# A fused attention and gated-MLP kernel on one NeuronCore: gated tiles' differences shared by two engines and stored a period later, weight sums made early, seven products in another order

## The chip, the cores and the metric

One NeuronCore of a Trainium2 chip runs the whole kernel in one launch. The metric is the device time of one execution in microseconds, lower is better. The engines have in-order queues of their own: TensorE (PE in the profile; PEld is its weight load), VectorE (DVE), ScalarE (ACT), GpSimd (POOL) and SyncE (SP), which issues nearly all DMAs.

## The reference

The output mixes an attention branch and a gated MLP of the same input `x` (2048 tokens, 512 features; 32 heads of 16; hidden width F = 1792), weighted by a gate per token:

```python
def _A_ref(x, wqkv, wo):
    ...
    scores = jnp.einsum("bhqd,bhkd->bhqk", q, k) * scale
    p = _softmax(scores, axis=-1)
    o = jnp.einsum("bhqk,bhkd->bhqd", p, v)
    return (lambda x, *d: x.transpose(*d))(o, 0, 2, 1, 3).reshape(B, S, D) @ wo

def _B_ref(x, w_gate, w_up, w_down):
    g = jnp.einsum("bsd,df->bsf", x, w_gate)
    u = jnp.einsum("bsd,df->bsf", x, w_up)
    h = _sigmoid(g) * u
    return jnp.einsum("bsf,fd->bsd", h, w_down)

x = A_x
g = _sigmoid((x * gate_w).sum(-1, keepdims=True))
a = _A_ref(x, A_wqkv, A_wo)
b = _B_ref(x, B_w_gate, B_w_up, B_w_down)
return g * a + (1 - g) * b
```

## The kernel before, in words

Everything is computed transposed (features on the 128 partitions, tokens along the free axis). Every dense product is three matmuls, of a high part and a low part of each factor (`split` makes them: a cast and a subtraction).

**Start** (to about 100 us): the first q, k and v, from `x` and `wqkv`.

**The main loop** has 256 periods (`for k in range(NPER)`), 16 to a pair of heads. In a period PE makes score tiles and tiles for the running maxima (L678, L292), 16 matmuls of values (L883, `values`), and 12 half-row matmuls of the *fill* (L163): all other dense products, one 512-column sum at a time (`filling`). VectorE takes a maximum over each tile of scores (L294, eight a period); ScalarE takes the exponentials (L680). GpSimd works off a list of steps, `later`: sums of values (L900), sums of the fill (`plus`, L540), splits of weights. Between the two halves of a fill sum stands a token (`turn`): an empty GpSimd instruction (L174) for which PE waits, and which comes to its turn when all earlier work of GpSimd is done. A table, `plans(k, kind, step)`, hangs further steps on the loads, on ScalarE or on VectorE of a period. `load_pair` loads the next pair's queries and keys at the start of every sixteenth period: eight DMAs, 1.5 MB. SP's issues wait for semaphores in its own order, too.

**Gated tiles.** The MLP's down projection is a two-by-two block product by the Strassen–Winograd scheme: seven products in place of eight, for each half of 1024 output columns. Its left factors are hidden tiles h (sigmoid written by a tanh) and four differences of them. `plan_quad(i, c, k0)` hangs one group of four tiles on the periods from k0 = 143 + 16 i + 8 c on: four loads of gate (tag `hg`, 2 buffers) and up tiles (`hu`, 5 buffers), tanh on ScalarE, a product on VectorE (`hid_mult`, L745), and `quad_steps`: four in-place subtractions on GpSimd through `later` (L737). Each result is stored to `op_d` (`hid_out`, L727) by a DMA that is issued directly behind its step. The last group (`last_quad`) runs in the tail. The last subtraction, tile 3 minus tile 2, writes tile 3, whose own store was issued a period earlier.

**End of the loop** (periods 240 to 255): no more maxima; first down weights (`first_weights`, A11 and A12) and the first four left factors are loaded and split.

**The tail**: per half, PRODUCTS `A11, A12, A22, S1, S2, S4, S3`, each 7 × 6 matmuls (L1175) with left factors that are loaded (`op_load`, 9 ahead) and split (`op_split`, 4 ahead: cast L102 on ScalarE, subtraction L105 on VectorE). The S weights are sums of blocks of `w_down`: `w_split` makes them on GpSimd at the start of the tail (L1014 to L1020, four of 256 columns for each of seven row blocks) and splits five blocks each time. `after` combines products on VectorE (L1105), and GpSimd multiplies with the gate (`scaled`, L1096) and adds an early part (`plus`, L1093). Then eight output tiles follow (`heads_out`: product with `wo`, L150, an addition on VectorE L1133, the store); `heads_load` and `heads_split` prepare attention's factors. `denominators` inverts the softmax sums in pieces of 32×64 (L840): one half at periods 144 to 216, the other in steps 18 to 36 of the tail.

Of the kernel before, what the change touches and what calls it, by code (L numbers as in the profile page):

```python
# [24 lines left out]
P = 128  # L25
# [20 lines left out]
def gated_mix(ctx, tc, x, xT, wqk, wv, wo, w_gate, w_up, w_down, gate_w, out):  # L46
# [28 lines left out]
    g_d = dram.tile([2, NS, 4, 32], F32, name="g_d")  # L75
    rec_d = dram.tile([P, 512], F32, name="rec_d")
# [124 lines left out]
    gwb = xp.tile([P, D], F32, name="gwb")  # L201
# [531 lines left out]
    def quad_steps(i, c, u):  # L733

        def minus(a, b, to, n):
            def step(engine):
                engine.tensor_tensor(u[to], u[a], u[b], ALU.subtract)  # L737
                hid_out(c, n, i, u[to])
            return step
# [4 lines left out]
    def hid_mult(i, c, j, g, u):  # L744
        dve.scalar_tensor_tensor(u, g, 1.0, u, op0=ALU.add, op1=ALU.mult)  # L745
        if j in OUT:
            hid_out(c, OUT[j], i, u)

    def plan_quad(i, c, k0):
        u, g = [None] * 4, [None] * 4  # L750
        for j, (f, ci) in enumerate(quad(i, c)):
            def load(a, j, f, ci):
                to = (g, u)[a]
                to[j] = keep.tile([P, 512], F32, name=f"h{'gu'[a]}{i}{c}{j}", tag="hu" if a else "hg",
                                  bufs=5 if a else 2)
                hid_load(a, f, ci, to[j])
            k = k0 + 2 * j
            plans(k, "load", lambda j=j, f=f, ci=ci: load(0, j, f, ci))
            plans(k + 1, "load", lambda j=j, f=f, ci=ci: load(1, j, f, ci))
            for a in range(2):  # L760
                plans(k + 1 + a, "act", lambda j=j, a=a: hid_tanh(g[j], slice(a * 256, (a + 1) * 256)))
            plans(k + 3, "dve", lambda j=j: hid_mult(i, c, j, g[j], u[j]))
        for off, step in zip((6, 8, 9, 10), quad_steps(i, c, u)):
            plans(k0 + off, "load", lambda step=step: later.append((1.3, lambda: step(pool))))

    for i in range(HF):
        for c in range(2 if i + 1 < HF else 1):
            plan_quad(i, c, 143 + 16 * i + 8 * c)

    def g_rows(a, g):  # L770
# [4 lines left out]
        for k in range(4):  # L775
            sp.dma_start(g_d[a, :, k, :], mt[32 * k:32 * k + NS, :])

    def g_chunks(a):
# [8 lines left out]
    plans(134, "load", lambda: [sp.dma_start(gwb[64 * i:64 * i + 64, :], g_chunks(0)[2 * i:2 * i + 2].unsqueeze(0).to_broadcast(  # L787
        [32, 2, 512])) for i in range(2)])
# [4 lines left out]
    A11, A12, S1, S4 = [cells(c) for c in (1, 3, 0, 2)]  # L793

    def first_weights(f):
        raw = keep.tile([P, 2, 256], F32, name=f"wf{f}", tag="wr", bufs=2)
        sp.dma_start(raw, w_down.rearrange("(a f p) d -> f p a d", a=2, p=P)[f, :, :, :256])

        def step():
            for a, block in enumerate((A11, A12)):  # L800
                split(*block[f], raw[:, a], dve, dve)
        return step

    seq = [(half, n, f) for half in range(2) for n in range(7) for f in range(HF)]
    raws, ops = {}, {}

    def op_load(m):
        if m < len(seq):
            half, n, f = seq[m]
            raws[m] = keep.tile([P, 512], F32, name=f"op{m}", tag="hu", bufs=5)  # L810
            sp.dma_start(raws[m], op_d[half, n, f])
# [13 lines left out]
    for f in range(HF):  # L825
        def load(f=f):
            step = first_weights(f)
            plans(NPER - 9 + f, "dve", step)
        plans(NPER - 10 + f, "load", load)
# [386 lines left out]
```

## Time and profile before

| | |
|---|---|
| median of 3 runs (range) | 1814.97 us (1812.5 to 1815.58) |
| the profiled execution: its own time / its span | 1817.36 us / 1815.6 us |
| mean granted TensorE clock | 0.971 |
| busy PE / DVE / ACT / POOL | 1721.3 / 1545.9 / 1409.6 / 1048.6 us |
| main loop's period with no hindrance | 5.57 us |
| main loop ends, tail begins | at about 1575.5 us of the span |

"x of y" figures of a stretch are the busy time of an engine in it; a row of waits names who waited, for whom, the sum, the count and the longest. The clock is the share that the throttle granted.

### The profile page before, as it was taken

What the parts mean: (1) busy time and instruction counts of PE and PEld (TensorE: products, weight loads), DVE (VectorE), ACT (ScalarE), POOL (GpSimd) and SP (SyncE); (2) the same over time, 40 slices, a digit from 0 to 9 for tenths busy, and PEclk for the clock granted to TensorE, in tenths of its full rate; (3) what the DMA queues carried; (4) which work ended last, traced back from release to release, by engine and by line L of the source; (5) the groups of instructions that cost most, each with busy time, mean ns of one, the idle gap of its engine ahead of it and who ended that gap; (6) DMA issues with size and microseconds to landing.
All of it is one profiled execution on the core that took longest, in us unless ns stands there. A gap on an engine that the chain in (4) does not pass through costs nothing.

```text
span 1815.6 us, 35561 instructions
## 1 busy us (share of the span) xinstructions
PE 1721.3 (95%) x12401; PEld 1056.3 (58%) x12401; DVE 1545.9 (85%) x2528; ACT 1409.6 (78%) x2833; POOL 1048.6 (58%) x1013
## 2 busy tenths in 40 slices
PE   9999999999999999999999898989899899868797
PEld 7756666655556666655555454545455454446585
DVE  7988888888899999999899898979799796769564
ACT  4288888998888888888999797979798788743141
POOL 1044566456666666666666776767676777352312
PEclk9999999999999999999999999989899899988898
DMA  7522555474655645574556566675656565557763
GB/s 233 129 60 70 157 179 182 129 227 134 192 135 172 169 154 159 162 197 142 147 183 181 167 188 179 182 205 181 175 185 176 169 217 178 177 186 230 224 199 115
DMA packets 173589, 309.88 MB, mean 171 GB/s; under 512 B 28576, under 2 KB 37536, under 8 KB 170528
## 3 DMA queue, kind: packets, MB, share of 16 engines
q1 hardware_dynamic: 165792, 292.91, 54.0%
q10 hardware_dynamic: 7616, 14.68, 2.6%
q8 instruction: 98, 1.61, 0.4%
q14 instruction: 83, 0.68, 0.1%
HBM read 179.31 MB, written 128.20 MB: 169 GB/s over the span
## 4 chain that ended last, share of the span: by engine, by line
PE 76%; DVE 8%; DMA 7%; POOL 4%; issue 3%; ACT 2%; SPq 0%; POOLq 0%; DVEq 0%; ACTq 0%
PE dn L163 25%; PE sm L883 23%; PE sm L292 13%; DVE stat L294 4%; PE st L678 4%; PE sm L678 4%; DMA op_d<-hu 2%; PE st L292 2%; PE sm L1175 2%; PE st L150 1%; DVE ops L105 1%; PE st L642 1%; ACT p L680 1%; DVE hu L745 1%; DMA ks<-k_d 1%
## 5 line engine op out<-in xcount | busy, mean ns | idle before, releaser
L294 DVE TENSOR_REDUCE stat<-sm 128x1 f32<-128x512 f32 x1313 | 847.8, 681 | 155.6 <-PE sm L678 107.3
L680 ACT ACTIVATE p<-sm 128x512 f32<-128x512 f32 x1027 | 609.5, 624 | 51.6 <-PE st L678 34.7
L680 ACT ACTIVATE p<-st 128x512 f32<-128x512 f32 x1019 | 611.6, 644 | 6.4 <-PE st L678 6.3
L292 PE MATMUL sm<-ks,qs 48*128 48x512 f32 x1313 | 525.0, 437 | 5.8 <-DVE stat L294 5.3
L883 PE MATMUL sm<-p,v 128*17 128x512 f32 x4016 | 487.5, 603 | 0.0
L294 DVE TENSOR_REDUCE stat<-st 128x1 f32<-128x512 f32 x735 | 479.6, 680 | 1.0 <-PE st L292 1.0
L678 PE MATMUL sm<-qs,ks 64*128 64x512 f32 x1027 | 431.0, 422 | 2.6 <-ACT p L680 2.6
L678 PE MATMUL st<-qs,ks 64*128 64x512 f32 x1019 | 429.2, 422 | 0.1
L292 PEld LDWEIGHTS sm<-ks,qs 48*128 48x128 f32 x1313 | 240.9, 185 | 280.0 <-DVE stat L294 227.9
L900 POOL TENSOR_TENSOR sum<-sum,part 128x512 f32<-128x512 f32 x224 | 290.8, 1298 | 128.6 <-PE sm L678 118.1
L292 PE MATMUL st<-ks,qs 48*128 48x512 f32 x735 | 290.6, 395 | 0.0
L883 PEld LDWEIGHTS sm<-p,v 128*17 128x17 f32 x4016 | 93.8, 97 | 235.1 <-issue 161.5
L888 ACT ACTIVATE part<-sm 128x512 f32<-128x512 f32 x214 | 128.1, 599 | 115.1 <-issue 66.6
L678 PEld LDWEIGHTS st<-qs,ks 64*128 64x128 f32 x1019 | 189.4, 186 | 32.1 <-issue 3.4
L678 PEld LDWEIGHTS sm<-qs,ks 64*128 64x128 f32 x1027 | 190.5, 186 | 12.2 <-issue 5.1
L540 POOL TENSOR_TENSOR chain<-chain,chain 128x512 f32<-128x512 f32 x96 | 124.8, 1300 | 96.9 <-PE sm L678 70.7
L540 POOL TENSOR_TENSOR had<-chain,had 128x512 f32<-128x512 f32 x96 | 123.3, 1284 | 36.5 <-PE sm L678 15.3
L292 PEld LDWEIGHTS st<-ks,qs 48*128 48x128 f32 x735 | 137.2, 187 | 1.4 <-ACT p L680 0.4
L737 POOL TENSOR_TENSOR hu<-hu,hu 128x512 f32<-128x512 f32 x52 | 67.3, 1294 | 61.6 <-DMA op_d<-hu 57.5
L102 ACT ACTIVATE ops<-op 128x512 fp32r<-128x512 f32 x94 | 54.8, 626 | 60.3 <-PE sm L1175 24.2
L105 DVE TENSOR_TENSOR ops<-op,ops 128x512 fp32r<-128x512 f32 x94 | 76.8, 847 | 19.2 <-ACT ops L102 18.2
L606 ACT ACTIVATE chain<-dn 128x512 f32<-128x512 f32 x128 | 86.5, 675 | 0.0
(875 smaller groups left out, 3361.7 us busy)
## 6 DMA issues: line engine op xcount, KB each, us to landing
op<-op_d SPq DMA_DIRECT2D x98, 256.0 KB
op_d<-hu SPq DMA_DIRECT2D x91, 256.0 KB
had<-gu_d SPq DMA_DIRECT2D x84, 256.0 KB
gu_d<-had SPq DMA_DIRECT2D x84, 256.0 KB
gu_d<-side SPq DMA_DIRECT2D x56, 256.0 KB
hg<-gu_d SPq DMA_DIRECT2D x52, 256.0 KB
hu<-gu_d SPq DMA_DIRECT2D x52, 256.0 KB
pv_d<-sum SPq DMA_DIRECT2D x32, 256.0 KB
```

What stands on the lines that cost most here:

```text
L105: return lo.tensor_tensor(l, src, h.bitcast(F32), ALU.subtract)
L163: mm = pe.matmul(self.o, a[rows], b[rows], start=(self.n == 0), stop=(self.n == 2 * len(self.ops) - 1))
L292: pe.matmul(t, qs[r:r + KM, qt * P:(qt + 1) * P], ks[r:r + KM, g * 512:(g + 1) * 512], start=True, stop=True)
L294: dve.tensor_reduce(stat[half][:, b, qt % 8, g:g + 1], t, axis=AX.X, op=ALU.max)
L540: pool.tensor_tensor(to, u, w, ALU.add)
L606: leave = lambda e, o: act.activation(e, o, AF.Copy)
L678: pe.matmul(o, ks[r:r + KR, (kt + a) * P:(kt + a + 1) * P], qs[r:r + KR, q0:q0 + 512], start=True, stop=True)
L680: act.activation(pt[:, 2 * a + c, :], o, AF.Exp, scale=DH ** -0.5)
L737: engine.tensor_tensor(u[to], u[a], u[b], ALU.subtract)
L883: pe.matmul(o[32 * c:32 * c + VW, :], v[:, 2 * k % 16 + a, h * VW:(h + 1) * VW], pts[c // 2][:, 2 * a + c % 2, :], start=(a == 0), stop=(a ...
L888: act.activation(e, o, AF.Copy)
L900: pool.tensor_tensor(s, s, e, ALU.add)
```

## The change

1. Of the four differences, two are made on VectorE (T1, T2) and two on GpSimd (T3, T4), by another scheme of in-place steps (a step `(to, a, b)` is u[to] = u[a] − u[b]); the group starts four periods earlier. Every store is hung on the next period's loads.
2. The sums of down weights are made on GpSimd in periods 42 to 73 and stored (`wc_d`); `w_split` now only splits one block, 512 columns at a time, ScalarE and GpSimd.
3. The products are reordered to `A11, S2, S3, S1, S4, A22, A12`, with one VectorE addition less per pair; the output tiles that a product completes follow one product later, and six of them end the program.
4. Denominators: first half at periods 122 to 143, a quarter in periods 249 to 255, a quarter in steps 4 to 13 of the tail. The gate's row tile moves into `hu`, which gets a sixth buffer.

```diff
-        return [minus(1, 0, 1, 3), minus(2, 1, 2, 4), minus(2, 0, 0, 6), minus(3, 2, 3, 2)]
+    T1, T2, T3, T4 = (1, 1, 0), (1, 2, 1), (0, 1, 0), (2, 3, 1)
...
+        def store(k, n, j):
+            plans(k0 + k, "load", lambda: hid_out(c, n, i, u[j]))
+
+        def sub(k, engine, step, n):
+            def run():
+                minus(engine, u, *step)
+                plans(now[0] + 1, "load", lambda: hid_out(c, n, i, u[step[0]]))
+            if engine is dve:
+                plans(k0 + k, "dve", run)
+            else:
+                plans(k0 + k, "pool", lambda: later.append((1.3, run)))
+        for j, (at, mult) in enumerate(((0, 3), (3, 5), (4, 7), (6, 10))):
...
+            plans(k0 + mult, "dve", lambda j=j: gated(j, g, u))
+            if j in OUT:
+                store(mult + 1, OUT[j], j)
+        sub(6, dve, T1, 3)
+        sub(8, dve, T2, 4)
+        sub(10, pool, T3, 6)
+        sub(11, pool, T4, 2)
...
-            plan_quad(i, c, 143 + 16 * i + 8 * c)
+            plan_quad(i, c, 139 + 16 * i + 8 * c)
+    def plan_combos(f, k):
...
+            op(a22, a21, a22, ALU.add)
+            op(a21, a11, a21, ALU.subtract)
+            op(a11, a22, a11, ALU.subtract)
+            op(a12, a12, a11, ALU.subtract)
...
+    for f, k in enumerate((42, 46, 49, 51, 61, 69, 73)):
+        plan_combos(f, k)
...
-    PRODUCTS = ["A11", "A12", "A22", "S1", "S2", "S4", "S3"]
+    PRODUCTS = ["A11", "S2", "S3", "S1", "S4", "A22", "A12"]
...
+    HEADS = {(0, "S4"): [(2, 2), (2, 3)], (0, "A22"): [(2, 0), (2, 1)], (0, "A12"): [(0, 2), (0, 3)],
+             (1, "A11"): [(0, 0), (0, 1)], (1, "S4"): [(3, 2), (3, 3)],
+             (1, "A12"): [(3, 0), (3, 1), (1, 2), (1, 3), (1, 0), (1, 1)]}
```

On SP, around a `load_pair` of the main loop (the rows `ks` are its last four; `hu113` is tile 3 of one group, `hu110` its tile 0, `hu20x` the next group). Before:

```order
L252 DMA ks0_103<-k_d_74 16x2048
L542 DMA gu_d_75<-chain12_13_13182 128x512
L524 DMA had03_00_13185<-gu_d_75 128x512
L902 DMA pv_d_76<-sum10_1_12695 128x512
L727 DMA op_d_78<-hu110_12624 128x512
L727 DMA op_d_78<-hu113_13061 128x512
L721 DMA hg201_13288<-gu_d_75 128x512
L542 DMA gu_d_75<-had03_00_13185 128x512
L524 DMA had03_02_13343<-gu_d_75 128x512
L727 DMA op_d_78<-hu113_13061 128x512
```

And now:

```order
L253 DMA ks0_104<-k_d_74 16x2048
L543 DMA gu_d_75<-chain12_13_13282 128x512
L972 DMA pv_d_76<-sum10_1_12801 128x512
L525 DMA had03_00_13284<-gu_d_75 128x512
L722 DMA hg203_13388<-gu_d_75 128x512
L543 DMA gu_d_75<-had03_00_13284 128x512
L525 DMA had03_02_13442<-gu_d_75 128x512
L722 DMA hu203_13459<-gu_d_75 128x512
L728 DMA op_d_78<-hu201_13162 128x512
L543 DMA gu_d_75<-had03_00_13284 128x512
L728 DMA op_d_78<-hu202_13304 128x512
```

The two stores of one group's tile 3 (plain, then as a difference) stood behind the pair's loads; now a group's tile 1 after T1 and its tile 2 stand there, and all stores of the group before are ahead of them.

On GpSimd, at the same place. Before:

```order
L900 TENSOR_TENSOR sum10_1_12695<-sum10_1_12695,part175_13203 128x512
L737 TENSOR_TENSOR hu110_12624<-hu112_12912,hu110_12624 128x512
L540 TENSOR_TENSOR had03_00_13185<-chain03_00_13264,had03_00_13185 128x512
L737 TENSOR_TENSOR hu113_13061<-hu113_13061,hu112_12912 128x512
L446 TENSOR_TENSOR chain1_3r_13187<-chain1_3r_13187,chain1_10r_13189 128x256
```

And now:

```order
L970 TENSOR_TENSOR sum10_1_12801<-sum10_1_12801,part175_13302 128x512
L447 TENSOR_TENSOR chain1_3r_13286<-chain1_3r_13286,chain1_10r_13288 128x256
L447 TENSOR_TENSOR chain1_10r_13288<-chain1_10r_13288 128x256
L447 TENSOR_TENSOR chain1_10r_13288<-chain1_10r_13288,chain1_3r_13286 128x256
L541 TENSOR_TENSOR had03_00_13284<-chain03_00_13365,had03_00_13284 128x512
```

No subtraction of a gated tile stands here any more: T1 and T2 of this group are on VectorE, T3 and T4 came two and three periods earlier.

On VectorE, at the end of the program (`ops` are left factors, `c`, `d`, `e`, `p` before and `y`, `z`, `p` now are combinations; `st1` and `st0` are the banks of the output tiles). Before:

```order
L105 TENSOR_TENSOR o3_3_20177<-ot3_3_20150,o3_3_20177 128x512
L1105 TENSOR_TENSOR d10_19846<-st2_67,d10_19846 128x512
L1105 TENSOR_TENSOR e10_19924<-st2_67,e10_19924 128x512
L1105 TENSOR_TENSOR d11_19848<-sm2_71,d11_19848 128x512
L1105 TENSOR_TENSOR e11_19926<-sm2_71,e11_19926 128x512
L1133 TENSOR_TENSOR c1110_19761<-st1_66,c1110_19761 128x512
L1133 TENSOR_TENSOR c1111_19767<-st0_65,c1111_19767 128x512
```

And now:

```order
L106 TENSOR_TENSOR ops96_20184<-op97_20153,ops96_20184 128x512
L1179 TENSOR_TENSOR p10_19674<-st2_67,p10_19674 128x512
L1179 TENSOR_TENSOR p11_19676<-sm2_71,p11_19676 128x512
L1202 TENSOR_TENSOR y10_19778<-st1_66,y10_19778 128x512
L1202 TENSOR_TENSOR y11_19780<-st0_65,y11_19780 128x512
```

Two additions instead of four follow the last product, no attention factor is split shortly ahead of it, and six output tiles instead of eight follow it.

More of the change, by code (lines that the diff above doesn't have):

```diff
@@ L763, in plan_quad, with load @@
[L763 to L764 removed]
+        def load(a, j):
+            f, ci = quad(i, c)[j]
+            to = (g, u)[a]
+            to[j] = keep.tile([P, 512], F32, name=f"h{'gu'[a]}{i}{c}{j}", tag="hu" if a else "hg", bufs=6 if a else 2)
+            hid_load(a, f, ci, to[j])
+        def store(k, n, j):
+            plans(k0 + k, "load", lambda: hid_out(c, n, i, u[j]))
@@ L1028, in wo_split, with w_load, w_split @@
         split(late["wo"][:, 0, k:k + 2, :], late["wo"][:, 1, k:k + 2, :], late.pop(("wo", k)), act, pool)
+    def w_load(name, f0):
+        raw = late[name, f0] = keep.tile([P, min(4, HF - f0), 256], F32, name=f"wl{name}{f0}", tag="ev", bufs=2)
+        weight_load(name, raw, f0)
+    def w_split(name, f0):
+        weight_split(name, late.pop((name, f0)), f0, act, pool)
     def last_quad(i, c):
-        two = [keep.tile([P, 2, 512], F32, name=f"hl{a}", tag="ev", bufs=2) for a in range(2)]
-        u = [two[j // 2][:, j % 2] for j in range(4)]
+        u = [keep.tile([P, 512], F32, name=f"hul{j}", tag=("sum", "part")[j % 2], bufs=2) for j in range(4)]
         g = {}
@@ L1187, in gated_mix @@
             m += HF
-            after(half, n, o)
-        for c, t, ks in HEADS[half]:
-            heads_out(c, t, ks)
+            after(half, name, o)
+            for c, t in HEADS.get((half, name), ()):
+                heads_out(c, t, range(2 if (c, t) in EARLY else 0, KT))
 def kernel(A_x, A_wqkv, A_wo, B_x, B_w_gate, B_w_up, B_w_down, gate_w):
```

259 lines of the change are left out of this document (143 added, 116 removed).

## The prediction, on record before the changed kernel ran

> **What bounds the kernel now.** I read the page's first part, then the stretches of the span, then who waits for whom where PE is not full, then the timeline and the chain at those places.
>
> ```profile
> PE 1721.3 (95%) x12401; PEld 1056.3 (58%) x12401; DVE 1545.9 (85%) x2528; ACT 1409.6 (78%) x2833; POOL 1048.6 (58%) x1013
> ```
>
> PE is the bound over all; at most some 95 us are idle, and more is lost where the clock sinks. The stretches below are 16 periods of the main loop each (rows 1 to 7), the loop's last 13 periods (row 8) and the tail (row 9); columns are length, busy PE, PEld, DVE, ACT, POOL (with counts), granted clock, DMA share, GB/s.
>
> ```profile
> 805.50:895.00 89.50, 89.50 (x707) 53.78 (x705) 80.77 (x138) 80.15 (x162) 60.98 (x57) 1.00 0.52 150
> 895.00:986.60 91.60, 91.50 (x706) 53.12 (x704) 87.17 (x145) 85.48 (x177) 69.20 (x62) 1.00 0.57 171
> 986.60:1088.10 101.50, 94.38 (x706) 53.84 (x704) 91.10 (x147) 85.58 (x178) 73.60 (x65) 0.97 0.62 184
> 1088.10:1190.50 102.40, 95.08 (x710) 53.76 (x712) 91.72 (x147) 85.84 (x178) 73.29 (x65) 0.97 0.63 182
> 1190.50:1292.10 101.60, 94.90 (x708) 54.19 (x709) 88.47 (x142) 85.63 (x177) 73.13 (x65) 0.95 0.64 183
> 1292.10:1395.10 103.00, 94.91 (x708) 53.97 (x706) 88.41 (x141) 85.73 (x177) 72.87 (x65) 0.95 0.62 180
> 1395.10:1498.80 103.70, 95.12 (x710) 54.09 (x711) 87.59 (x141) 85.81 (x177) 75.28 (x66) 0.95 0.66 197
> 1498.80:1575.50 76.70, 68.67 (x498) 34.12 (x496) 52.07 (x89) 64.53 (x134) 42.55 (x36) 0.96 0.55 176
> 1575.50:1815.60 240.10, 193.57 (x737) 145.10 (x736) 159.94 (x229) 81.62 (x155) 71.17 (x62) 0.89 0.60 191
> ```
>
> The same some 706 matmuls take 89.5 us without gated tiles, 91.6 with the first group's, and 101.5 to 103.7 in five stretches; the tail has PE busy for 193.6 of 240.1 us. The waits (this list from 930 to 1585 us) name what happens in the five:
>
> ```profile
> POOL hu L737 <- DMA op_d<-hu: 57.5, 12, 8.6
> PE dn L163 <- POOLq L174: 36.1, 7, 6.8
> ```
>
> GpSimd waits before a subtraction of gated tiles for a store to land, and PE waits for GpSimd's token. The timeline shows one of the five, with one row of the chain (the fifth):
>
> ```profile
> 1089.73 1.75 DVE L745 SCALAR_TENSOR_TENSOR hu<-hg,hu 128x512 f32<-128x512 f32 x1
> 1091.19 0.58 SPq L252 DMA_DIRECT2D ks<-k_d  x1
> 1093.85 1.62 SPq L727 DMA_DIRECT2D op_d<-hu  x2
> 1102.30 1.26 POOL L737 TENSOR_TENSOR hu<-hu,hu 128x512 f32<-128x512 f32 x1 [8.03 <-DMA op_d<-hu]
> 1095.15 7.02 DMA op_d<-hu
> 1107.30 1.29 DVE L294 TENSOR_REDUCE stat<-sm 128x1 f32<-128x512 f32 x2 [6.66 <-PE sm L292]
> ```
>
> VectorE ends tile 3 at 1091.5; its store is issued behind the pair's loads (their last at 1091.19) and takes 7.02 us; the in-place subtraction on GpSimd must wait for it 8.03 us; token, PE and then VectorE stand.
>
> **The change, part by part.**
>
> *The stall at the pair's loads.* In the new scheme no step overwrites tile 3. Counted modulo 16 periods, in the group whose steps straddle a `load_pair` (period 0) T1 is in period 1 on VectorE, its store in 2, T2 (which overwrites the stored tile) at the end of 3, T3 and T4 on GpSimd in 5 and 6; T4 overwrites tile 2, stored at the start of 3. Between each store and the step that overwrites it lie about two periods or more, 11 us, against 7.02 for a store in the worst jam. So this wait goes; late next is then VectorE's own work.
>
> *Two subtractions per group on VectorE.* They stand ahead of VectorE's maxima, on which PE's banks hang. No period shows a subtraction there; the nearest rows are the products of the same size (L745), with periods around them:
>
> ```profile
> L745 DVE SCALAR_TENSOR_TENSOR hu<-hg,hu 128x512 f32<-128x512 f32 x47 | 56.0, 1192 | 0.2
> 1259.28 0.85 DVE L745 SCALAR_TENSOR_TENSOR hu<-hg,hu 128x512 f32<-128x512 f32 x1
> 1257.90:1263.50 5.60, 5.60 (x49) 3.40 (x52) 5.50 (x10) 5.14 (x12) 5.44 (x6) 1.00 0.34 125
> 1282.16 1.23 DVE L745 SCALAR_TENSOR_TENSOR hu<-hg,hu 128x512 f32<-128x512 f32 x1
> 1280.60:1286.50 5.90, 5.90 (x47) 3.22 (x45) 5.90 (x10) 5.47 (x12) 4.92 (x5) 1.00 0.43 117
> 1293.67 1.75 DVE L745 SCALAR_TENSOR_TENSOR hu<-hg,hu 128x512 f32<-128x512 f32 x1
> 1292.10:1298.50 6.40, 5.90 (x46) 3.24 (x44) 6.40 (x10) 5.44 (x12) 4.06 (x4) 1.00 1.01 199
> ```
>
> A step of 0.85 us is free (the period stays 5.6 us), one of 1.23 lengthens it by 0.3, one of 1.75 by 0.8: VectorE's rest is 5.50 − 0.85, 5.90 − 1.23 and 6.40 − 1.75, each time 4.65 us, so its slack is 0.9 us a period. The mean of the 47 is 1.19 us, nearest to the middle row, which would be 0.3; since short steps give nothing back for long ones, I take 0.4 per step. The bounds are 0 and 0.85. A stretch of 16 periods then has 8 products and 4 subtractions: 89.5 + 12 × 0.4 = 94.3 us. The five stretches sum to 512.2; five times 94.3 is 471.5: **−40.7 us** (with 0: −64.7; with 0.85, 99.7 a stretch: −13.7). The stretch from 895.0, with no stall, goes from 91.6 to 94.3: **+2.7** (0 to +8). GpSimd loses two of four such steps, which gains nothing: it is not the bound once the wait is gone.
>
> *Denominators.* The trace has these pieces as
>
> ```profile
> L840 DVE RECIPROCAL den<-den 32x64 f32<-32x64 f32 x16 | 8.7, 546 | 0.5
> ```
>
> Sixteen of them now stand in periods 123 to 138. One of 0.55 us fits into the slack of 0.9, but six of those periods carry the token gate's steps on VectorE already; 6 × 0.5 gives **+3** (0 to +5). The place they leave cost nothing: 0.55 is below the slack, and no product stood beside them.
>
> *Weight sums made early.* 28 GpSimd steps of 128×256; one of the same size and kind, and the stretch of 32 periods in which they are to stand:
>
> ```profile
> 1103.52 0.72 POOL L446 TENSOR_TENSOR chain_3r<-chain_3r,chain_10r 128x256 f32<-128x256 f32 x1
> 324.40:502.70 178.30, 178.30 (x1410) 107.94 (x1408) 157.68 (x265) 160.13 (x321) 102.59 (x107) 1.00 0.57 170
> ```
>
> 28 × 0.72 = 20 us beside 102.6 busy of 178.3: hidden, **0**, and so are its 28 DMAs of 256 KB at a DMA share of 0.57. If GpSimd's spare third were gone, the fill's weights would come late, and PE with them.
>
> *The loop's end.* Two waits of the same kinds go, a gate tile whose load was issued late because SP stood before a store (at 1510 to 1515), and a store under a subtraction (1550 to 1554):
>
> ```profile
> ACT hg L724 <- DMA hg<-gu_d: 3.4, 1, 3.4
> POOL hu L737 <- DMA op_d<-hu: 8.6, 1, 8.6
> ```
>
> PE feels about 3.4 of the first, and of the second the 3 to 4 us by which its token is late: −7. Four reciprocals of double width, about 1 us each by the row above, come into its last periods: +4. Together **−3** (−8 to +5).
>
> *The tail.* Its floor by PE follows from the chain's rows where PE runs unhindered, the values at its start, and the last step:
>
> ```profile
> 1578.57 1.91 PE st L883 x16
> 1724.10 11.56 PE sm L1175 x51
> 1795.40 15.54 PE st L150 x60
> 1811.03 0.69 DVE e L1133
> 1673.18 11.02 issue
> 1690.54 8.84 issue
> L105 DVE TENSOR_TENSOR ops<-op,ops 128x512 fp32r<-128x512 f32 x94 | 76.8, 847 | 19.2 <-ACT ops L102 18.2
> POOL late L1014 <- DVE wohl L105: 17.7, 6, 4.1
> ACT xh L102 <- POOL late L1014: 19.4, 7, 7.0
> ```
>
> 2 × 7 × 42 = 588 product matmuls at 11.56 / 51 = 0.227 us are 133.3; 132 for the output tiles at 15.54 / 60 = 0.259 are 34.2; with 1.9 at the start and 4.6 behind 1811.03, 174.0 of the 240.1 us. The other 66 are waits of three sorts: the round ScalarE, VectorE, GpSimd of the weight sums (the last two rows) in the first 55 us; VectorE's full queue after it; and waits around the output tiles, where those of half 0 stood behind the last product and eight additions of GpSimd (chain, 1673 to 1707). All three are edited: the sums leave, 35 splits of weights leave VectorE for GpSimd, and the tiles stand behind products whose sums are older. What is late next is VectorE between steps 4 and 28: 24 splits at 0.847, eight reciprocals at 0.546, four attention factors at two steps of some 0.75 and four additions at 0.69 come to 20.3 + 4.4 + 6.0 + 2.8 = 33.5 us for 24 × 1.36 = 32.6 us of PE, ahead of which ScalarE must cast (18.2 us of waits over 94 splits). I leave 12 us for it and for loads behind other loads: 186, **−54** (3 left: −63; 30 left: −36).
>
> Sum: −40.7 + 2.7 + 3 + 0 − 3 − 54 = −92 us. The profiled execution took 1817.36 us, 2.4 above the median of the three runs; off the median, 1814.97 − 92 = **1723 us**.
>
> **The rivals.**
>
> *VectorE pays full price (about 1750 us).* If each of the twelve steps costs what the one of 1.75 us does, a stretch takes 99.7: five gain 13.7 instead of 40.7. For it: in eight periods VectorE would be busy for 8 × 4.65 + 6 × 1.2 = 44.4 of 44.6 us, and four of the six steps stand in neighbouring periods, where none can be made up for. Against it: the mean of 47 products costs less, and GpSimd has less to do. The Trainium skill's page "SBUF — State Buffer" (section "Who interferes with whom") says that a VectorE instruction with two SBUF inputs contends with a GpSimd instruction that reads SBUF, and that whichever comes second blocks until the first is done; by it a subtraction that moves to VectorE may always meet a GpSimd step, and this rival would be the rule. The spread of the rows (0.85 to 1.75 us for one instruction) agrees that something holds it at times, not that it always does.
>
> *The tail keeps half its waits (about 1753 us).* The tail's 191 GB/s over 240.1 us must now pass in 186: its DMA share rises from 0.60 to 0.77, SP's loads stand in one queue with stores that wait for VectorE, and loads come late; 42 us left instead of 12. For it: the stores of output tiles now stand among the loads. Against it: pair loads ran at a share of 1.01 (row at 1292.1).
>
> *The stall changes its place (about 1763 us).* Behind `load_pair` GpSimd still adds fill tiles whose loads (`had`) are issued there; if one is as late as the store was, the five stalls of some 8 us stay. Against it: in the trace these additions come a period after the load, and GpSimd's own work fills most of that.
>
> *Slower than before.* T2 waits on VectorE for the store of the tile that it overwrites, and every wait there stops PE's banks at once, in all 13 groups, not in five. It decides from 92 / 13 = 7.1 us a group; at the 8.03 us that GpSimd waited, 13 × 8.03 = 104 us are lost: 1827. Against it: that store has two periods, 11 us, which even the jam's 7.02 us leave free, and only six of the 13 groups straddle a pair's loads.
>
> **How the numbers follow.** Chances: forecast as summed 0.54 (its own range 1708 to 1740), full price on VectorE 0.14, tail half 0.18, stall elsewhere 0.09, slower 0.05. Two of the middle ones together still end below 1795, so faster is 0.94, slower 0.05, and 0.01 for within 0.2% (about what a measurement of this kernel can tell from no change). The range of 1700 to 1766 takes in the three middle cases and the better bounds of the steps' price and the tail; some 0.17 lies outside, most of it above.
>
> **What would show it.** In the profile after: the five stretches at about 94 us, clock 1.00, no wait of GpSimd for `op_d<-hu`, no token wait above 2 us; L740 on VectorE twice a group at some 1.2 us; the tail at about 186 us with PE above 90% and no stretch of 10 us without matmuls. Wrong it would be by VectorE waiting on a DMA before L740, by stretches of 99 us or more at a full clock, by PE waiting for `ops` in the tail, or by GpSimd waiting for `had`.

## The result, and the profile after

| | before | after |
|---|---|---|
| median (range) | 1815.28 us (1812.5 to 1821.39, 4 runs) | 1742.6 us (1739.23 to 1746.9, 4 runs) |
| ratio | | 0.9597, 95% interval 0.9564 to 0.9629 |
| profiled execution: own time / span / clock | 1817.36 / 1815.6 us / 0.971 | 1739.23 / 1737.4 us / 0.995 |

The change takes 73 us off; 92 were forecast. The two profiled spans differ by 78.2 us (the profiled run of the changed kernel is the fastest of its four), and the stage figures below add up to that. Lines have moved: the maxima are now L295, score tiles and exponentials L679 and L681, the fill's matmuls L164, values L953, products of gated tiles L737 and their subtractions L740 on both engines, splits L103 and L106, tail products L1252, output tiles L151.

The first part of the page after shows that PE's share went from 95% to 98% of a shorter span, and that VectorE's went from 85% to 89% with the same work:

```profile
PE 1698.2 (98%) x12401; PEld 1039.0 (60%) x12401; DVE 1549.0 (89%) x2499; ACT 1408.3 (81%) x2818; POOL 1042.1 (60%) x1007
```

The stretches after, cut at the starts of the same periods as before: the first group of gated tiles, the five stretches that held the stall, the loop's end, and the tail from the last values on (columns: length, busy PE, PEld, DVE, ACT, POOL with counts, granted clock, DMA share, GB/s):

```profile
905.20:998.00 92.80, 92.41 (x709) 52.78 (x710) 90.74 (x145) 85.84 (x177) 68.16 (x61) 1.00 0.66 194
998.00:1090.60 92.60, 92.42 (x707) 52.79 (x706) 90.44 (x145) 85.89 (x177) 68.06 (x61) 1.00 0.69 201
1090.60:1183.20 92.60, 92.47 (x710) 52.73 (x712) 90.46 (x145) 85.94 (x177) 68.08 (x61) 1.00 0.69 201
1183.20:1275.80 92.60, 92.43 (x710) 52.74 (x712) 90.43 (x145) 85.91 (x177) 68.08 (x61) 1.00 0.67 201
1275.80:1368.20 92.40, 92.20 (x706) 52.81 (x704) 90.16 (x145) 85.74 (x177) 68.64 (x61) 1.00 0.69 200
1368.20:1462.90 94.70, 92.99 (x710) 52.61 (x712) 91.22 (x146) 85.72 (x177) 70.28 (x62) 1.00 0.68 207
1462.90:1534.70 71.80, 68.30 (x510) 34.23 (x508) 55.74 (x81) 66.16 (x135) 36.29 (x32) 1.00 0.52 168
1534.70:1737.40 202.70, 176.55 (x725) 134.69 (x724) 139.53 (x181) 75.73 (x134) 76.90 (x53) 0.97 0.73 231
```

With the starts of the values' matmuls as marks in both traces, the difference falls into these places:

| place | before | after | measured | predicted |
|---|---|---|---|---|
| up to period 40 | 313.3 | 312.7 | −0.6 | 0 |
| periods 40 to 79 (weight sums) | 223.3 | 231.0 | +7.7 | 0 |
| periods 80 to 121 | 235.1 | 235.2 | +0.1 | 0 |
| periods 122 to 143 (denominators) | 123.3 | 126.3 | +3.0 | +3 |
| periods 144 to 159 (first group) | 91.6 | 92.8 | +1.2 | +2.7 |
| five stretches, periods 160 to 239 | 512.2 | 464.9 | −47.3 | −40.7 |
| loop's end, to the last values | 79.7 | 71.8 | −7.9 | −3 |
| tail, from the last values on | 237.1 | 202.7 | −34.4 | −54 |

The loop did a little better than forecast. The tail gave 20 us less, and 7.7 us more are spent in a part that the forecast had called hidden.

In the loop the waits that the prediction quoted are gone. The list of PE's waits from 905 to 1535 us has one for a token. In GpSimd's list for the same time no subtraction waits for `op_d<-hu`; two additions of the fill (L541) are put down to such a store, 2.5 us in all. VectorE's longest waits there are for PE:

```profile
PE dn L164 <- POOLq L175: 1.3, 1, 1.3
POOL had L541 <- DMA op_d<-hu: 2.5, 2, 1.3
DVE stat L295 <- PE sm L679: 10.5, 22, 0.8
```

The tail's waits (engine, line, what was waited for: sum, times, longest) show that ScalarE now stands for op loads, which were 4.4 us before, and PE for split operands:

```profile
ACT ops L103 <- DMA op<-op_d: 34.2, 19, 3.6
PE st L1252 <- DVE ops L106: 8.2, 14, 1.8
PE st L1252 <- ACT ops L103: 5.1, 5, 1.7
```

The timeline around 376 us shows the new wait (start, length, engine, line; "q" marks a queue that issues DMAs; in brackets the idle time before and what ended it):

```profile
374.78 0.70 ACT L607 ACTIVATE side<-dn 128x512 f32<-128x512 f32 x1
376.03 1.13 SPq L796 DMA_DIRECT2D wc_d<-wc  x2
377.10 0.39 ACTq L375 DMA_DIRECT2D xh<-t_d  x1
377.20 0.46 SPq L525 DMA_DIRECT2D had<-s_d  x1
377.71 4.02 SPq L789 DMA_DIRECT2D wc<-in_w_down_dram  x5
379.05 0.37 ACTq L375 DMA_DIRECT2D xl<-t_d  x1
379.54 0.60 ACT L958 ACTIVATE part<-sm 128x512 f32<-128x512 f32 x1 [4.06 <-POOL side L541]
380.68 0.79 PE L679 MATMUL sm<-qs,ks 64*128 64x512 f32 x1 [2.92 <-ACT p L681]
```

ScalarE ends its step at 375.48, then issues a load of `xh` only at 377.10 and one of `xl` at 379.05; its next step starts at 379.54, and PE stands for ScalarE's exponential. The row names GpSimd's addition as what ended ScalarE's wait; that had ended at 379.26, but the load that stands ahead of the step in ScalarE's order was issued at 379.05 itself. The 1388 DMA issues of this trace use eight semaphores, 173 or 174 issues each, and no issue on a semaphore starts before the DMA ahead of it on that semaphore has landed. For `xh` that was a store of weight sums, issued at 370.77 and landed at 377.08; for `xl` a load of `had`, issued at 373.68 and landed at 379.03. At 470.01 and 472.25 us it is the same (the DMAs ahead landed at 469.99 and 472.23), and period 67 takes 7.36 us in place of 5.57. PE is idle for 2.92 us in period 51 and for 1.24 in period 67; most of the other 3.5 us is work of PE at a lowered clock, 0.50 from 379.4 to 386.2 us (rows in the last section), which also makes period 52 last 6.48 us.

### The profile page after: what moved, and what is told of

It reads as the page before. It is cut to its first block, busy times and chain, and to the rows that moved or that the text cites. A ratio compares the mean times of both kernels' runs of the same rounds, so it can differ in the third digit from the quotient of the medians.

```text
span 1737.4 us, 35521 instructions
## 1 busy us (share of the span) xinstructions
PE 1698.2 (98%) x12401; PEld 1039.0 (60%) x12401; DVE 1549.0 (89%) x2499; ACT 1408.3 (81%) x2818; POOL 1042.1 (60%) x1007
## 4 chain that ended last, share of the span: by engine, by line
PE 76%; DVE 10%; DMA 5%; ACT 5%; issue 2%; POOL 1%; SPq 0%; DVEq 0%; ACTq 0%; POOLq 0%
PE dn L164 24%; PE sm L953 23%; PE sm L293 14%; DVE stat L295 6%; PE sm L679 4%; PE st L679 4%; ACT p L681 3%; DMA op<-op_d 2%; PE st L293 2%; PE st L643 1%; PE st L151 1%; DVE ops L106 1%; PE sm L1252 1%; DVE hu L737 1%; DMA hpl<-hp_d 1%
## 5 line engine op out<-in xcount | busy, mean ns | idle before, releaser
L295 DVE TENSOR_REDUCE stat<-sm 128x1 f32<-128x512 f32 x1313 | 847.0, 680 | 95.0 <-PE sm L679 82.2
L681 ACT ACTIVATE p<-sm 128x512 f32<-128x512 f32 x1027 | 612.7, 622 | 12.6 <-PE sm L679 8.9
L681 ACT ACTIVATE p<-st 128x512 f32<-128x512 f32 x1019 | 609.0, 641 | 1.5 <-PE st L679 1.4
L953 PE MATMUL sm<-p,v 128*17 128x512 f32 x4016 | 480.9, 596 | 0.0
L295 DVE TENSOR_REDUCE stat<-st 128x1 f32<-128x512 f32 x735 | 479.1, 679 | 0.2 <-PE st L293 0.2
L679 PE MATMUL sm<-qs,ks 64*128 64x512 f32 x1027 | 428.6, 420 | 5.4 <-ACT p L681 5.2
L679 PE MATMUL st<-qs,ks 64*128 64x512 f32 x1019 | 426.8, 420 | 0.0
L953 PEld LDWEIGHTS sm<-p,v 128*17 128x17 f32 x4016 | 93.1, 97 | 232.2 <-issue 157.8
L679 PEld LDWEIGHTS st<-qs,ks 64*128 64x128 f32 x1019 | 187.9, 184 | 33.7 <-issue 3.4
L541 POOL TENSOR_TENSOR chain<-chain,chain 128x512 f32<-128x512 f32 x96 | 124.0, 1291 | 128.2 <-ACT p L681 47.1
L679 PEld LDWEIGHTS sm<-qs,ks 64*128 64x128 f32 x1027 | 189.7, 185 | 16.7 <-ACT p L681 7.6
L541 POOL TENSOR_TENSOR had<-chain,had 128x512 f32<-128x512 f32 x96 | 123.8, 1290 | 42.0 <-PE sm L679 23.9
L103 ACT ACTIVATE ops<-op 128x512 fp32r<-128x512 f32 x94 | 55.7, 624 | 66.4 <-DMA op<-op_d 34.2
L106 DVE TENSOR_TENSOR ops<-op,ops 128x512 fp32r<-128x512 f32 x94 | 84.4, 931 | 27.6 <-ACT ops L103 27.4
L541 POOL TENSOR_TENSOR side<-side,side 128x512 f32<-128x512 f32 x32 | 41.3, 1292 | 69.6 <-PE sm L679 68.3
```

Of the source, the lines that this page charges most:

```text
L103: act.activation(h, src, AF.Copy)
L106: return lo.tensor_tensor(l, src, h.bitcast(F32), ALU.subtract)
L295: dve.tensor_reduce(stat[half][:, b, qt % 8, g:g + 1], t, axis=AX.X, op=ALU.max)
L541: pool.tensor_tensor(to, u, w, ALU.add)
L679: pe.matmul(o, ks[r:r + KR, (kt + a) * P:(kt + a + 1) * P], qs[r:r + KR, q0:q0 + 512], start=True, stop=True)
L681: act.activation(pt[:, 2 * a + c, :], o, AF.Exp, scale=DH ** -0.5)
```

## The experiments

Each was timed beside the kernel before on the same chip; ratios are to it. Stages are read from one profile each.

**e1: one index in the kernel before.**

```diff
-        return [minus(1, 0, 1, 3), minus(2, 1, 2, 4), minus(2, 0, 0, 6), minus(3, 2, 3, 2)]
+        return [minus(1, 0, 1, 3), minus(2, 1, 2, 4), minus(2, 0, 0, 6), minus(3, 2, 2, 2)]
```

> The kernel before, in which the fourth subtraction of each group writes tile 2 instead of tile 3; nothing else is changed, and stores are still issued at once. Theory A (the stall was that one overwriting of tile 3 behind its store in the jam): tile 2's last store is issued before the pair's loads, so GpSimd's wait for op_d<-hu falls from 57.5 us to under 5, the five stretches of 101.5 to 103.7 us come near the 91.6 of the first group's, and the time falls by some 5 x 10.5 to 58 us, to about 1757 to 1765. Rival B (what cured it is that stores are issued a period later, or the subtractions that left GpSimd): tile 2's own store waits in the same jam, the stretches stay above 100 us and the time stays within 10 us of 1815.

Measured: 1765.8 us (1764.93 to 1768.21), ratio 0.9734 (0.9714 to 0.9755). The first two of the five stretches, the tail, and GpSimd's only wait for such a store left between 930 and 1520 us:

```profile
985.30:1078.70 93.40, 92.34 (x706) 52.99 (x704) 90.24 (x147) 85.37 (x177) 73.66 (x65) 1.00 0.66 199
1078.70:1172.00 93.30, 92.34 (x706) 52.92 (x704) 90.70 (x147) 85.67 (x178) 73.34 (x65) 1.00 0.68 199
1529.00:1762.90 233.90, 188.79 (x725) 141.90 (x724) 156.46 (x225) 78.51 (x149) 69.42 (x61) 0.90 0.61 194
POOL hu L737 <- DMA op_d<-hu: 4.0, 1, 4.0
```

The five stretches add up to 467.7 us instead of 512.2: −44.5 of the change's −47.3 come from where the fourth subtraction writes. All four are still on GpSimd here, and stores are issued at once. The last 3 us are not told apart: the changed loop itself took 464.4 to 467.9 us for these stretches in the profiles in which it was not edited (the change, e3 to e8 and e12). The tail is the old one.

**e11: stores at once in the changed kernel.**

```diff
-                plans(now[0] + 1, "load", lambda: hid_out(c, n, i, u[step[0]]))
+                hid_out(c, n, i, u[step[0]])
...
-                store(mult + 1, OUT[j], j)
+                plans(k0 + mult, "dve", lambda j=j: hid_out(c, OUT[j], i, u[j]))
```

> The changed kernel with every store of a gated tile or of a difference issued with its step, not a period later. Theory A (the cure is that the fourth subtraction writes another tile): stretches stay at 92.6 us within 1.5, the time within 5 us of 1742. Rival B (the late stores are needed: SyncE now stands before a store until VectorE or GpSimd has made it, and gate loads behind it come late): stretches of 95 us or more, the time 1755 or more.

Measured: 1739.59 us (1738.83 to 1741.95), ratio 0.9589 (0.9569 to 0.961), not to be told from the change's 0.9597. The first of the five stretches:

```profile
996.60:1089.60 93.00, 92.56 (x708) 52.96 (x706) 90.85 (x145) 85.93 (x177) 68.12 (x61) 1.00 0.67 201
```

All five take 467.5 us, inside the 464.4 to 467.9 just told. Theory A holds: no effect of the late stores shows, neither a cure nor a cost.

**e2: all four subtractions on GpSimd.**

```diff
-        sub(6, dve, T1, 3)
-        sub(8, dve, T2, 4)
+        sub(6, pool, T1, 3)
+        sub(8, pool, T2, 4)
```

> The changed kernel with all four subtractions of a group on GpSimd, at the same periods. Theory (a step on VectorE costs 92.6 - 89.5 = 3.1 us over 12 steps, 0.26 us each, and GpSimd is not the bound): four steps fewer in each stretch, 92.6 becomes about 91.5, 26 steps in all give -6.8 us, the time is about 1736. Rival (GpSimd is the cover that was needed): its busy time rises from 68 to about 73 us a stretch, it waits for the store of tile 1 before T2 and PE waits for its token, stretches of 95 us or more, the time 1755 or more.

Measured: 1735.37 us (1729.61 to 1740.25), ratio 0.9574 (0.9551 to 0.9597). Two of the five stretches:

```profile
996.20:1087.70 91.50, 91.39 (x706) 53.38 (x704) 86.41 (x141) 85.39 (x178) 72.81 (x65) 1.00 0.68 203
1271.10:1362.60 91.50, 91.37 (x706) 53.14 (x704) 86.52 (x141) 85.29 (x177) 72.95 (x65) 1.00 0.67 203
```

Four steps fewer on VectorE take 0.7 to 1.1 us off each of the first four stretches, some 0.24 a step, near the 0.26 that 92.6 − 89.5 over 12 steps had said; GpSimd at 73 of 91.5 us is still no bound. The fifth does not follow: 95.6 us here, 94.0 to 97.0 where the loop is unedited. Over the whole kernel the intervals of this ratio and the change's overlap; the four stretches carry the verdict. In them, sharing the subtractions with VectorE cost time instead of saving it.

**e3: weight sums without GpSimd's steps.**

```diff
-            op(a22, a21, a22, ALU.add)
-            op(a21, a11, a21, ALU.subtract)
-            op(a11, a22, a11, ALU.subtract)
-            op(a12, a12, a11, ALU.subtract)
```

> The changed kernel without the 28 GpSimd steps of the early weight sums; their loads and stores stay, so the sums are wrong. Theory L (ScalarE's loads xh, xl stand at 375.5 to 379.1 and 470.4 to 472.3 us until an earlier DMA, of the weight sums or behind them, has landed): the two long periods stay, 10.4 and 7.4 us instead of 5.57 within 1 us, the time within 3 us of 1742. Theory G (GpSimd's steps make the period long): both periods are 5.6 us, the time falls by 7 us to 1735.

Measured: 1740.86 us (1737.78 to 1743.21), ratio 0.9594 (0.9573 to 0.9615). Both long periods are 5.57 and 5.58 us, as theory G said, but the run does not tell the theories apart: with no steps between them, all 28 loads and stores of the sums came to stand early in SyncE's order, at 54 to 90 us (the change has five of them there), so ScalarE's loads no longer met them either. At 54 to 90 us they came ahead of a load that PE waits for (`qs<-max_d`, 4.7 us), and the loop began 6.5 us later in the profile (first values at 96.1 us, in the change at 89.6), which ate the gain.

**e4: three pairs of weight sums moved.**

```diff
-    for f, k in enumerate((42, 46, 49, 51, 61, 69, 73)):
+    for f, k in enumerate((42, 46, 82, 90, 61, 98, 73)):
```

> The changed kernel with three of the seven pairs of weight sums (those of periods 49, 51 and 69) moved to periods 82, 90 and 98, where ScalarE issues no loads. Theory L: the long periods at 374 and 469 us are gone and none comes elsewhere, -7.6 us, about 1735. Rival: the moved DMAs make VectorE's and GpSimd's loads of that part late, and the 7.6 us come back there: 1742.

Measured: 1739.04 us (1736.43 to 1739.97), ratio 0.9583 (0.9562 to 0.9603). Period 51 takes 6.39 us instead of 10.36, but 67 stays at 7.49: periods 40 to 79 take 226.1 us instead of 231.0. Moving the steps did not move all loads: two of a later pair were issued at 461.1 and 461.8 us, as soon as their buffers were free. ScalarE's load of `xh` then started at 467.74, right after the DMA ahead on its semaphore had landed at 467.66. That DMA ahead was an earlier load of ScalarE's own, issued at 459.76. Some 4.9 of the 7.7 us came back, less 0.9 by which periods 80 to 121 grew, and the miss agrees with theory L.

**e8: ScalarE's loads on SyncE's queue.**

```diff
-            act.dma_start(xs[:, k0:k0 + 2, cols].bitcast(F32), t_d[n, a, c]...
+            sp.dma_start(xs[:, k0:k0 + 2, cols].bitcast(F32), t_d[n, a, c]...
```

> The changed kernel with the 28 loads of xh and xl that ScalarE issues put on SyncE's queue. Theory L (ScalarE stands before its own DMA until the DMA ahead of it on the same semaphore has landed; everything of ScalarE stands behind it): the periods at 374 and 469 us come down from 10.4 and 7.4 to under 6.2 us, -6 us or more, about 1736. Theory G (GpSimd's weight sums make the period long): they stay long, 1742.

Measured: 1744.9 us (1741.83 to 1746.59), ratio 0.9613 (0.9596 to 0.9631). At both places the periods are 5.57 us, with the GpSimd steps of the sums where they were:

```profile
370.00:400.00 30.00, 30.00 (x242) 18.35 (x235) 26.23 (x45) 26.58 (x55) 18.09 (x20) 1.00 0.88 297
POOL chain_2r L447 <- DMA wc<-in_w_down_dram: 6.1, 1, 6.1
PE dn L164 <- POOLq L175: 4.2, 1, 4.2
```

PE is busy for all of 370 to 400 us with GpSimd's steps in place, so theory G falls as the cause of these two long periods, and theory L is shown. The time did not fall, because now SyncE stands before those loads: period 56 takes 11.4 us (the second and third rows: GpSimd waits for a load behind them, and PE for GpSimd's token), and periods 128 and 129 take 8.55 and 7.12.

**e5 and e12: less to load in the tail, then less to split.**

```diff
     def op_load(m):
         if m < len(seq):
             half, n, f = seq[m]
+            if m > 9 and m % 2:
+                raws[m] = raws[m - 1]
+                return
```

e12 also leaves the split of these operands out:

```diff
     def op_split(m, engine=act):
+        if 9 < m < len(seq) and m % 2:
+            ops[m] = ops[m - 1]
+            return
```

> The changed kernel, in which from the tenth on every second load of a product operand in the tail is left out (44 of 98, 11.5 of some 47 MB) and its split reads the tile before, so the products are wrong; the work of all engines is the same. Theory D (what the tail has above the sum of PE's work are op loads that land 7 to 10 us after their issue at DMA shares of 0.9 and more): the tail falls from 202.7 to some 186 to 190 us, the time to about 1727 to 1731. Rival V (VectorE's splits, at 931 ns instead of 847, bound it): the tail stays within 4 us of 202.7, the time within 5 of 1742.

> As e5, and the split of every second operand (44 casts on ScalarE, 44 subtractions on VectorE) is left out too: the product uses the operand before. What e5 left above the sum of PE's work, 191.7 - 174 = 17.7 us, is then split: VectorE loses 44 x 0.93 = 41 of its 140 us. If VectorE's and ScalarE's queue is what remained, the tail falls from 191.7 to some 178 to 182 us, the time to about 1718. If it is the lowered clock (PE's work takes 6 to 7 us more than at full speed) and the waits around the output tiles, it stays within 4 us of 191.7, the time near 1730.

Measured: e5 1730.78 us (1730.3 to 1731.97), ratio 0.9538 (0.9524 to 0.9553); e12 1718.93 us (1716.25 to 1720.77), ratio 0.9482 (0.9458 to 0.9506). The tail of e5 and its waits for op loads; e12's tail from 0.9 us after its last values (1536.1 us):

```profile
1537.50:1729.20 191.70, 175.47 (x725) 136.95 (x724) 140.51 (x179) 74.02 (x134) 77.36 (x53) 0.95 0.56 182
ACT ops L103 <- DMA op<-op_d: 4.5, 3, 3.7
1537.00:1715.90 178.90, 167.80 (x720) 135.58 (x712) 102.97 (x134) 51.35 (x90) 74.94 (x53) 0.97 0.60 194
```

Half the op loads away take 11.0 us off the tail (202.7 to 191.7), and the waits for them fall from 34.2 to 4.5 us. Half the splits away take another 11.9 (to 179.8). So theory D and the queue of ScalarE and VectorE each hold about 11 of the 31.7 us that the tail has, from the last values on, above its floor of 171.0 (the prediction's 174.0 less the 3.0 us by which its window began earlier); 8.8 are left. One profile's tail is known to some 5 us only (see e7), but the ratios say nearly the same: they fall by 0.0059 and 0.0056, 10.7 and 10.2 us of 1815. Which of the two engines holds the second part e12 does not say.

**e6: a third of the low parts on GpSimd.**

```diff
-        split(h, l, raws.pop(m), engine, dve)
+        split(h, l, raws.pop(m), engine, pool if m > 13 and m % 3 == 0 else dve)
```

> The changed kernel with the low parts of every third product operand of the tail (28 of 98 splits) on GpSimd instead of VectorE. Theory V: VectorE loses 28 x 0.93 = 26 us of its 139.5 in the tail, the tail falls by 10 us or more, the time to about 1730. Theory D: operands are late before they reach VectorE, so the tail stays within 4 us, or is longer, since GpSimd takes 1.29 us for such a step: 1740 to 1750.

Measured: 1750.31 us (1748.63 to 1753.38), ratio 0.9647 (0.9628 to 0.9666), slower than the change by its median; the two intervals just touch. The tail, and what PE waited for:

```profile
1535.10:1749.00 213.90, 180.48 (x725) 138.40 (x724) 127.25 (x153) 76.22 (x134) 114.08 (x81) 0.94 0.70 219
PE st L1252 <- POOL ops L106: 9.2, 5, 3.5
PE dn L1252 <- POOL ops L106: 7.7, 3, 6.9
```

VectorE lost 12 us of work and the tail grew by 11.2: the two rows of PE's waits say that GpSimd hands these operands over later than PE wants them. So less work of VectorE alone does not shorten the tail; theory V fails in this form. That the way of each operand from its landing to PE is the bound fits, but the run does not prove it: VectorE's other steps also grew longer beside the busier GpSimd (a remaining split 0.97 us instead of 0.90, the product L1142 for attention's factors 1.15 instead of 0.78), and this part was not separated.

**e7: the loads of attention outputs spread.**

```diff
-    for half, at in enumerate((((12, 17), (12, 20), (17, 23), (20, 26), (30, 36), (33, 39)),
-                               ((60, 65), (60, 68), (65, 71), (68, 74), (72, 78), (75, 81)))):
+    for half, at in enumerate((((12, 17), (14, 20), (18, 23), (22, 27), (30, 36), (33, 39)),
+                               ((58, 63), (62, 67), (66, 71), (70, 75), (76, 82), (80, 86)))):
```

> The changed kernel with the loads of attention outputs and factors (ot, rb) in the tail spread: steps 12, 14, 18, 22 instead of 12, 12, 17, 20 in half 0, and 58, 62, 66, 70, 76, 80 instead of 60, 60, 65, 68, 72, 75 in half 1, and their splits with them. Theory D: the jam at 1652 to 1690 us, where five pairs of these loads stand among the op loads, is thinner, op loads land sooner, the tail is 4 to 8 us shorter, about 1736. Rival (the sum of the bytes sets it, wherever they stand): within 2 us of 1742.

Measured: 1739.79 us (1738.13 to 1741.71), ratio 0.9587 (0.9572 to 0.9603): no difference to the change that the intervals show. Its tail took 195.8 us and its waits for op loads 17.3 instead of 34.2; but the same unedited tail took 198.4 to 208.9 us in the profiles of the change, e2, e3, e4, e8 and e11, so 195.8 is a hint only. In this profile period 67 took 9.72 us, which hid it in the total.

**e10: three edits together** (e2, e7, and the sums' periods as 42, 46, 76, 82, 90, 98, 106).

> The changed kernel with three edits together: all four subtractions on GpSimd, the weight sums of periods 49 to 73 moved to 76, 82, 90, 98 and 106, the loads of attention outputs spread in the tail. If their gains are of different places they add up: from 1742.6, -6 (steps), -7 (no DMA of the sums among ScalarE's loads from 366 to 480 us, both long periods gone), -6 (tail): about 1723. If the moved sums bring the wait elsewhere, about 1730.

Measured: 1727.88 us (1724.5 to 1729.45), ratio 0.9518 (0.9496 to 0.954), 0.8% below the change; only e12, which leaves work out, is faster. Of the expected parts the sums came near (periods 40 to 79 in 224.3 us instead of 231.0; between 366 and 480 us PE is busy for 113.67 of 114), though periods 80 to 121 grew by 1.0. The steps brought little: the five stretches took 463.3 us (462.0 in e2, 464.9 in the change). The tail took 199.5 us, 3 us less than the change's and inside the spread just told.

## Why the prediction was right or wrong, point by point

- **The number.** The case "as summed" had a range of its own, 1708 to 1740 us; 1742.6 lies just above it and inside the range of 1700 to 1766 that took in the rivals. It is as close as it is partly by luck: three stages of the loop did 13 us better than forecast (−6.6, −1.5, −4.9), which hid some of the 27 us by which the sums and the tail did worse (+7.7, +19.6).
- **The stall at the pair's loads.** Right, and narrower than told: the wait of GpSimd for the store of tile 3 is gone, and e1 shows that writing the last difference elsewhere cures it alone. The prediction had argued from the time between each store and the step that overwrites it; e11 shows no further gain from the period of delay. By the rows before and after, 35 of the 47.3 us were idle time of PE; the other 12 are the same matmuls at a granted clock of 1.00 instead of 0.95 to 0.97.
- **The price of VectorE's steps: the term was sized at 0.4 us, and it is 0.26.** A stretch is 92.6 us, not 94.3, which is the 6.6 us by which the five were better. The step that failed is "nearest to the middle row": the products changed their length too. Their row and that of the subtractions (engine, line: shortest, median, longest in ns, first and last start):

```profile
L745 DVE SCALAR_TENSOR_TENSOR hu<-hg,hu x52: 662/1176/1776, 906.4 to 1500.8; 128x512 f32<-128x512 f32 x52
L737 DVE SCALAR_TENSOR_TENSOR hu<-hg,hu x52: 673/1148/1529, 894.9 to 1492.5; 128x512 f32<-128x512 f32 x52
L740 DVE TENSOR_TENSOR hu<-hu,hu x26: 676/1070/1190, 912.8 to 1482.0; 128x512 f32<-128x512 f32 x26
```

  The first row is e1's, with products where they stood before; the other two are the change's. Those of 1.75 us, which made a period 6.45 us long twice in each of e1's stretches (93.4 us against e2's 91.5 with the same steps), do not occur in the change. The rival of the full price (99.7 us a stretch) is refuted, though its premise came true: every one of these steps meets a step of GpSimd (last section).
- **Denominators.** +3.0 measured, +3 predicted, in the periods named.
- **Weight sums: 0 predicted, +7.7 measured.** The step that failed is "hidden, and so are its 28 DMAs": cover was looked for in GpSimd's free third and in the mean DMA share. GpSimd was indeed no limit (e8 keeps its steps and has no long period there), but ScalarE issues 20 of its 28 loads in this part, and each stands until an earlier DMA on its semaphore has landed, with the exponentials behind it. Sums of DMA bytes over 178 us also hid that they come in lumps: five loads of 256 KB within 4 us at 377.7, when buffers came free. What the prediction named as late next (the fill's weights) was not.
- **The loop's end.** −7.9 instead of −3, inside its bounds (−8 to +5). Before, periods 242 and 249 took 9.75 and 8.41 us; after, 5.57 and 3.83. The four wide reciprocals cost less than the 4 us set against it (+2.5 in periods 252 to 254).
- **The tail: the mis-sized term.** −54 predicted, −34.4 measured. The predicted window begins 3.0 us ahead of the last values; in it the changed tail takes 205.7 us instead of 186. The floor of 174.0 took PE at full speed, 169.4 us of work and 4.6 at the end, but PE was busy for 179.5: 10.1 more. Half of that is the clock: three stretches of 3.4 us at a granted clock of 0.50, all with PE busy, make 5.1; what the other 5 are stays open. For waits 12 us were left, and 26.2 of idle time less 4.6 at the end make 21.6: 9.6 more. What was late next was named, and PE waits for `ops` as the prediction's sign of being wrong had it, but it was sized by VectorE alone; the runs show op loads behind other loads (11 us, e5) as large as the splits (11.9, e12). The waits for the weight sums (17.7 and 19.4 us before) are gone from the lists; how much of the 34.4 us each of the tail's three edits brought no run separates.
- **The rivals.** The tail that keeps half its waits was the nearest: of its reasons e5 shows the late loads, while no run tests whether the stores among them in SP's queue are to blame. Of its 42 us of waits and the forecast's 12 the 21.6 measured lie between; for the tail as a whole it said −24, ten from the measured −34.4 where the forecast is twenty off. The stall did not move to `had` loads: GpSimd waits for them 3.0 us in all between 905 and 1535 us, 1.2 at the longest. The slower case found nothing: no row has VectorE waiting for a DMA before L740.

## What to carry to other kernels

Before an in-place step, ask which transfer still reads the tile; one index that names another tile took 2.7% off the old kernel, where the whole change took 4.0%. Work that is moved "under" another stage needs cover on every queue that it touches, DMA semaphores included, and DMA that looks spread in a mean can arrive in lumps. A free share of an engine is not the same as short service: where operands are wanted just after they land, the slower engine lengthens the path even when it stands half idle.

## What the runs showed of the hardware that was not expected

**A VectorE step with two SBUF inputs lasts as long as GpSimd's neighbour makes it.** All 41 products of the kernel before between 900 and 1420 us overlap a step of GpSimd, and so do all 45 products and 22 subtractions on VectorE after. Who starts first decides. GpSimd first by 0.08 us, at 1293 us in the kernel before:

```profile
1293.59 1.28 POOL L737 TENSOR_TENSOR hu<-hu,hu 128x512 f32<-128x512 f32 x1
1293.67 1.75 DVE L745 SCALAR_TENSOR_TENSOR hu<-hg,hu 128x512 f32<-128x512 f32 x1
```

VectorE first by 0.26 us, at 1259 us:

```profile
1259.54 1.75 POOL L900 TENSOR_TENSOR sum<-sum,part 128x512 f32<-128x512 f32 x1
```

In the first pair VectorE's step takes 1.75 us, where the shortest take 0.66, and GpSimd's its usual 1.28; in the second VectorE's takes 0.85 (the prediction's row) and GpSimd's 1.75. Whoever came second took about as much longer as the other still had to run: VectorE's step ended 0.55 us after GpSimd's. The Trainium skill's page "SBUF — State Buffer" (section "Who interferes with whom") says so: the pair of ports is locked for a whole instruction, and issue order decides who blocks. The prediction read the spread as "at times, not always"; the traces agree with the page, and the price is what is left of GpSimd's step, not a fixed sum: over these 108 steps the time on VectorE is 0.66 to 0.69 us with nothing of GpSimd's step left at the start, and else what is left of it plus some 0.55.

**A DMA issue can stop a compute engine although its data are not wanted yet.** ScalarE stood 1.6 us before one issue and some 1.6 before the next (at 375.5 to 379.05), each time until 0.02 us after the landing of an unrelated DMA on the same semaphore, which took 6.3 and 5.4 us. The Trainium skill's page "DMA: Bandwidth & Descriptors" (section "Why a DMA increments its semaphore by 16 and not by 1") tells why two DMAs in flight must not share a semaphore; that an engine that also computes pays for it by standing is what this trace adds.

**The clock falls to half after a stretch that PE fills only by half.** Two such falls in the trace after, one in the loop and one in the tail, each with the 3.4 us ahead of it:

```profile
376.00:379.40 3.40, 1.75 (x13) 1.11 (x13) 2.48 (x4) 0.00 (x0) 2.00 (x3) 1.00 1.07 393
379.40:386.20 6.80, 5.52 (x27) 3.45 (x31) 3.01 (x6) 5.25 (x10) 1.48 (x2) 0.50 0.99 361
1676.50:1679.90 3.40, 1.86 (x6) 1.03 (x7) 2.70 (x6) 2.19 (x4) 0.00 (x0) 1.00 1.02 268
1679.90:1683.30 3.40, 3.40 (x10) 2.63 (x9) 1.21 (x2) 0.20 (x1) 0.00 (x0) 0.50 0.68 221
```

In the loop it was one pause of 2.92 us; in the tail several short ones, of at most 1.1 us, were enough. The falls at 1639.0 and 1693.6 us look alike (PE busy for 1.88 and 1.82 us of the 3.4 ahead). Not every thin stretch does it: from 1546.8 and from 1563.9 us PE was busy for 1.62 and 1.68 of 3.4 us, and the clock stayed at 1.00. What decides is not shown. Some waits of PE are so paid for a second time, and a sum of matmuls at full speed is a floor and not an estimate.

**The loads of attention outputs use half as many completions.** In the trace after, the 24 loads `ot` and `rb` of the tail complete by nine semaphore events each, the 98 op loads of the same 256 KB by 16. Between 1657 and 1666 us, where four of the former are in flight, landings follow each other by 1.9 to 2.2 us; behind them, op loads land 0.4 to 0.7 us apart. The Trainium skill's page "DMA: Bandwidth & Descriptors" (same section) says that a DMA runs on the largest number of engines up to 16 that divides the slowest dimension of both sides, and that the issuer posts the rest of the 16 in one write; the source here is 8 heads of 16 rows, so eight engines and nine events agree with it. Whether a source of 16 or 128 rows would shorten the tail's jam was not tried.
